# Three passes instead of two through the first expert's hidden blocks, fewer early weight tiles and fewer dummy matmuls

## The chip, the cores and the metric

The kernel runs on one core of one Trainium2 chip. The metric is device time in microseconds (us) of one execution, the median of several runs. One further execution is recorded by the hardware profiler, and all rows below come from that one.

## The reference, cut to what matters

```python
attn_out = _attn_ref(q, k, v, n_global, n_local)     # B=2, H=8, S=768, D=64
x = transpose(attn_out).reshape(1536, 512)           # tokens x model
x = _moe_ref(x, w_in, w_out)                         # d_ff = 2048
return _moe2_ref(x, w_gate, w_val, w_out2)           # d_ff = 1536

# _attn_ref: softmax(q k^T / 8 - slope * distance), keys kept if local (0 <= i - j < 96) or global (j < 8)
# _moe_ref:  h = x @ w_in;  g = h * tanh(softplus(h));  g @ w_out
# _moe2_ref: silu(x @ w_gate) * (x @ w_val) @ w_out
```

The weights are float64 and come as pairs of int32 words; the kernel turns them into float32 itself.

## The kernel before

**Stages.** The attention goes over 12 tiles of 128 tokens (6 for each of two batches), each in two halves of four heads. Then the first expert goes over 16 blocks of 128 hidden columns, then the second over 12. A chunk is 512 tokens, so there are three chunks (`NCH`). Every float32 operand of an expert's matmul is split in a high and a low part, and a product takes three matmuls (`PASSES`, `mm3`, L371).

**Attention, one half tile.** `transp` (L440) transposes q and k on TensorE into a PSUM bank of the pool `t_p`, and ACT or DVE evicts it to `kq`; `qk` (L469) makes the scores; `softmax` (L485) runs four biased minimum reductions on DVE (L499) and four exponentials on ACT (L329); `turn` (L528) transposes the exponentials through `t_p`, and ACT or DVE evicts them to `et`. Once for a tile, `spread` (L508) transposes the reciprocals through `t_p` into `rs`, and `pv` (L551) multiplies with the values into a bank of `t_p`. Of the eight PSUM banks the scores use banks 0 to 3, `t_p` banks 4 to 6, and `warm_p` bank 7 alone.

**Dummies.** `warm_up` (L590) makes `WARM` = 6 matmuls of 128x512 at the very start and `LATE` = 24 more of the lowest priority, which run wherever the planner sees TensorE free. All write bank 7.

**Weights.** `convert` (L392) loads one tile (512 KB from HBM), takes the absolute value of the high words on ACT (L404), runs four integer steps on DVE (L887 to L890), copies the high part to the tile on ACT or POOL (L352, L349) and subtracts for the low part on DVE (L362). A block of the first expert needs two tiles, `in` and `out`; a block of the second needs three. There are 13 slots `wa` from the start and 15 more, `wb`, once the attention's memory is given back (`switch`, L830). In the attention's loop `units_to(min(9, max(0, (s - 3)//2)))` (L827) writes nine conversions into the program, one for each two half tiles; all later ones are placed by `need` (L852), up to eight jobs ahead of their use.

**First expert.** `jobs_b` (L736) takes two blocks: `hidden` (24 matmuls, L681) into two banks `h`, then `mish` (L698: on ACT tanh, a table load, logarithm, a table load, tanh; on DVE a product and the split), then `out_b` (L759: 24 matmuls). The four output banks `y` are banks 4 to 7, given over when the attention is done (L841). The order is: blocks 0 to 7 for chunks 0, 1 and 2, then blocks 8 to 15 for chunks 0, 1 and 2 (`FA` = 8, L845). At the end of a chunk in the first pass the four `y` banks are copied to `st` and stored to `part1` in HBM (L779, L780); in the second they are loaded back (L782), added on DVE (L588) and split by POOL into the second expert's input. `st` has two slots, and two more (`sb`) after `switch`.

**Order.** Nothing runs in the order of the source. All operations go into `Plan` with assumed costs; `order` (L182) fills each engine's queue greedily, always with the ready operation of the lowest priority value, which is the due time worked back from its users. Engines then run these queues in order, each instruction waiting on its inputs. Copies that ACT, DVE or POOL can do are given to one of them there. A pool's buffers are handed out in the order of the source.

Of the kernel before, what the change touches and what calls it, by code (L numbers as in the profile page):

```python
# [13 lines left out]
ALU = mybir.AluOpType  # L14
# [205 lines left out]
def kernel(  # L220
# [14 lines left out]
    nc = tc.nc  # L235
# [6 lines left out]
    KD = DM // P  # L242
    CH = 512
    NCH = NTOK // CH
    FA = F1 // 2
    NWA = 13
    NWB = 15
    NST = 2
    WARM = 6
    LATE = 24  # L250
    EDGE = 104
    SPARE = 2500.0
    SCALE = -1.0 / float(D) ** 0.5
# [55 lines left out]
    sm_p = Pool(slots(asb, 3, [P, H], F32, "sm"))  # L309
    asb.tile([P, EDGE], I32, name="edge")  # L310

    asb_pools = [*raw_in.values(), e_p, sm_p, et_p, rb_p, xs_p, rs_p, t_p, warm_p]
    asb_fixed = [bias, bias0, kq, kg, mn, nt, nf, chk]

    def of_attention(o):
# [17 lines left out]
    def dve(emit, r, w, n=512, fast_=False):  # L333
        return op([("V", (150 if fast_ else 68) + (0.52 if fast_ else 1.045) * n, emit)], r, w)

    def dma(emit, r, w, kb=256, prio=None):
        return op([("S", 150 + kb * 4.2, emit)], r, w, lat=2000.0, prio=prio)
# [77 lines left out]
    def load(i, names="qk"):  # L415
        b, t = tiles[i]
        for nm, src in (("q", q), ("k", k), ("v", v)):
            if nm not in names:
                continue
            x = plan.buf(raw_in[nm])  # L420
            raws[nm, i] = x
            for hs in (slice(0, 4), slice(4, 8)) if i == 0 else (slice(0, H),):
                dma(lambda x=x, src=src, hs=hs: nc.sync.dma_start(
                    out=x.t[:, hs], in_=src[b, hs, t * P:(t + 1) * P, :].rearrange("h s d -> s h d")), [],
                    [(x, hf) for hf in range(hs.start // 4, hs.stop // 4)], kb=32 * (hs.stop - hs.start),
                    prio=-1e6 + hs.start + 9 * (nm == "v") if i == 0 else None)
# [160 lines left out]
    def tt(o, a, b_, op_):  # L587
        nc.vector.tensor_tensor(out=o, in0=a, in1=b_, op=op_)  # L588
# [13 lines left out]
    def setup():  # L602
        warm_up(WARM, LATE)
        load(0, "qk")
        op([("S", 154, lambda: nc.sync.dma_start(out=nt.t[:, 0:2], in_=n_global.bitcast(I32).partition_broadcast(P)))], [],
           [(nt, 0)], lat=3700.0, prio=-2e6)
        op([("S", 154, lambda: nc.sync.dma_start(out=nt.t[:, 2:4], in_=n_local.bitcast(I32).partition_broadcast(P)))], [],
           [(nt, 1)], lat=3700.0, prio=-2e6)
        load(0, "v")
        idb = Buf(t=ident)  # L610
        op([("G", 300, lambda: make_identity(nc, ident))], [], [(idb, 0)])
        op([("A", 1300, lambda: nc.scalar.preload_act_table_set(SET_EXP_TANH))], [], [(table, 0)])
        s0, s1 = plan.buf(e_p), plan.buf(e_p)
        v0 = lambda i, n: s0.t.rearrange("p a b -> p (a b)")[:, i:i + n]
        v1 = lambda i, n: s1.t.rearrange("p a b -> p (a b)")[:, i:i + n]
        rel_i, key_i = lambda: v0(0, 256).bitcast(I32), lambda: v0(256, 128).bitcast(I32)
        rel, key, neg, far = lambda: v0(384, 256), lambda: v0(640, 128), lambda: v0(768, 128), lambda: v1(0, 256)
        dist = (lambda: v1(256, 128), lambda: v1(384, 256))
        ng, nl = lambda: nf.t[:, 0:1], lambda: nf.t[:, 2:3]

        def iotas():
            nc.gpsimd.iota(rel_i()[:, 0:128], pattern=[[-1, 128]], base=128, channel_multiplier=1)
            nc.gpsimd.iota(rel_i()[:, 128:256], pattern=[[-1, 128]], base=0, channel_multiplier=1)
            nc.gpsimd.iota(key_i(), pattern=[[1, 128]], base=0, channel_multiplier=0)

        op([("G", 900, iotas)], [], [(s0, 0)])

        def distances():
            nc.vector.tensor_copy(rel(), rel_i())
            nc.vector.tensor_copy(key(), key_i())  # L630
            ts(neg(), rel()[:, 128:256], 0.0, ALU.is_lt, FAR, ALU.mult)
            tt(rel()[:, 128:256], rel()[:, 128:256], neg(), ALU.max)

        op([("V", 810, distances)], [(s0, 0)], [(s0, 1)])

        def masks():
            nc.vector.tensor_copy(nf.t, nt.t)
            ts(far(), rel(), nl(), ALU.is_ge, FAR, ALU.mult)
            tt(dist[1](), rel(), far(), ALU.max)
            ts(key(), key(), ng(), ALU.is_ge, FAR, ALU.mult)  # L640
            ts(key(), key(), nl(), ALU.max)
            tt(dist[0](), dist[1]()[:, 128:256], key(), ALU.min)
            nc.vector.tensor_copy(dist[1]()[:, 0:WG], key()[:, 0:WG])

        op([("V", 1800, masks)], [(nt, 0), (nt, 1), (s0, 1)], [(s1, 0), (nf, 0)])
        for o, c0, x, n in ((bias0, 0, dist[0], P), (bias, 0, dist[1], 2 * P), (bias, 2 * P, lambda: dist[1]()[:, 0:P], P)):
            for h in range(H):
                slope = 2.0 ** (-8.0 * (h + 1) / H)
                copy(lambda o=o, c0=c0, n=n, h=h: o.t[:, h, c0:c0 + n], x, [(s1, 0)], [(o, h)], scale=slope / SCALE, n=n)
# [109 lines left out]
    def out_b(kind, c, f, first, last, whole, g, w, ds):  # L759
        for d in ds:  # L760
            if first:
                ys[d] = plan.buf(y_p)
            y = ys[d]
            blk = slice(d * P, (d + 1) * P)

            def emit(y=y, blk=blk):
                if kind == 1:
                    mm3(y.t, lambda a: w.t[:, a, blk], lambda b: g.t[:, b, :], first, last)
                else:
                    mm3(y.t, lambda a: g.t[:, a, blk], lambda b: w.t[:, b, :], first, last)  # L770

            pe(emit, [(w, 0), (w, 1), (g, 0), (g, 1)], [(y, 0)], 3, CH, spare=SPARE)
            if not last:
                continue
            st = plan.buf(st_p)
            Y, T = [(y, 0)], [(st, 0)]
            if not whole:
                part, pk = (part1, p1) if kind == 1 else (part2, p2)
                copy(lambda st=st: st.t, lambda y=y: y.t, Y, T, scale=1.0 if kind == 1 else 0.5, psum_in=True, on="AV")  # L779
                dma(lambda st=st, d=d, part=part: nc.sync.dma_start(out=part[c, d], in_=st.t), T, [(pk, (c, d))])  # L780
            elif kind == 1:
                dma(lambda st=st, d=d: nc.sync.dma_start(out=st.t, in_=part1[c, d]), [(p1, (c, d))], T)  # L782
                dve(lambda st=st, y=y: tt(st.t, y.t, st.t, ALU.add), Y, T)
                ks = lambda a: [(xt[c], (a, d, t)) for t in range(CH // P)]
                copy(lambda d=d: xt[c].t[:, 0, d, :], lambda st=st: st.t, T, ks(0), on="G")
                arith(lambda d=d: xt[c].t[:, 1, d, :], lambda st=st: st.t,
                      lambda d=d: xt[c].t[:, 0, d, :].bitcast(F32), ALU.subtract, T + ks(0), ks(1), on="G")
            else:
                dma(lambda st=st, d=d: nc.sync.dma_start(out=st.t, in_=part2[c, d]), [(p2, (c, d))], T)
                dve(lambda st=st, y=y: nc.vector.scalar_tensor_tensor(out=st.t, in0=y.t, scalar=0.5, in1=st.t,  # L790
                                                                      op0=ALU.mult, op1=ALU.add), Y, T)
                r = c * CH + d * P
                dma(lambda st=st, r=r: nc.sync.dma_start(out=out[r:r + P, :], in_=st.t), T, [])


    setup()
    load(1)
    transp(0, 0)
    transp(0, 1)
# [2 lines left out]
    def units_to(n):  # L802
        while n_units[0] < min(n, len(units), freed[0] + room[0]):
            convert(n_units[0])
            n_units[0] += 1

    NS = 2 * NTL
    for s in range(NS + 2):
        i, hf = divmod(s, 2)
        if s < NS:  # L810
            if hf == 0:
                load_previous(i)
                if i + 1 < NTL:
                    load(i + 1, "v")
            qk(s)
            softmax(s)
            move_k(i, hf)
            if i + 1 < NTL:
                transp(i + 1, hf)
            if hf == 1 and i + 2 < NTL:  # L820
                load(i + 2)
        if 0 <= s - 1 < NS:
            turn(s - 1)
            if s % 2 == 0:
                spread(s // 2 - 1)
                pv(s // 2 - 1)
        units_to(min(9, max(0, (s - 3)//2)))  # L827
        if s == NS:
            flag()
    def switch():  # L830
# [11 lines left out]
       grow=[(w_p, wb_slots), (st_p, st_slots), (y_p, bank[4:8])])  # L842
    room[0] += NWB
    seq = []
    for fs, whole in ((range(0, FA), False), (range(FA, F1), True)):  # L845
        for c in range(NCH):
            seq += [(1, c, f, f == fs[0], f == fs[-1], whole) for f in fs]
    for fs, whole in ((range(0, F2 // 2), False), (range(F2 // 2, F2), True)):
# [281 lines left out]
```

## Time and profile before

| | us |
|---|---|
| median of 3 runs (669.0 to 670.03) | 669.59 |
| the profiled execution's own time | 668.81 |
| its span, first to last instruction | 667.0 |

The rows below are of that profiled execution. PE is TensorE's matmul side, PEld its weight loads, DVE VectorE, ACT ScalarE, POOL GpSimd, SPq the DMA issues of SyncE. The recorded durations of matmuls overlap, so the distance of starts, or a piece of the chain divided by its count, tells the cost of one. "Idle" is time before an instruction, with what ended it.

### The profile page before, as it was taken

Reading aid. Unit: us, or ns where it says so; the run is one execution under the profiler, and the core shown is the slowest. Engines: PE = TensorE matmul, PEld = TensorE weight load, DVE = VectorE, ACT = ScalarE, POOL = GpSimd, SP = SyncE. Lnnn points to the kernel's source line nnn. Section 1 sums busy time; section 2 is a strip of 40 time slices with the busy share of each in tenths; the row PEclk is TensorE's granted clock in tenths of the full one; section 3 lists DMA queues with packets and bytes.
Section 4 is the critical chain, followed back from the end, with each engine's and each line's share of the span. In section 5 each row is a group of like instructions: output and inputs, shape, how many; then the busy total and the mean of one; then the engine's idle time right before and its main releaser. Section 6 shows DMA issues by size and latency. Waiting matters only on the chain.

```text
span 667.0 us, 9142 instructions
## 1 busy us (share of the span) xinstructions
PE 652.8 (98%) x3343; PEld 535.9 (80%) x3343; DVE 410.5 (62%) x831; ACT 351.1 (53%) x636; POOL 109.7 (16%) x168
## 2 busy tenths in 40 slices
PE   8998999999999999999999999999999999999996
PEld 6876778878888888888888888888888888888884
DVE  5788887888678685797688877222842223323313
ACT  6999997878766776867685333212521211111111
POOL 4343542112111110150251410000000000000000
PEclk9999999999999999999999999999999999999999
DMA  8677641433325234243132224100400300300301
GB/s 197 171 174 179 168 129 63 127 127 130 117 70 179 73 132 153 94 143 124 51 127 93 97 70 142 72 1 1 148 10 16 111 0 17 111 0 17 110 1 68
DMA packets 80068, 63.58 MB, mean 95 GB/s; under 512 B 48272, under 2 KB 68752, under 8 KB 80016
## 3 DMA queue, kind: packets, MB, share of 16 engines
q1 hardware_dynamic: 80016, 62.93, 30.8%
q8 instruction: 28, 0.46, 0.3%
q14 instruction: 24, 0.20, 0.1%
HBM read 53.48 MB, written 9.44 MB: 94 GB/s over the span
## 4 chain that ended last, share of the span: by engine, by line
PE 89%; ACT 5%; DVE 2%; DMA 2%; issue 1%; SPq 0%; ACTq 0%; DVEq 0%
PE bank L373 78%; PE bank L562 3%; PE bank L480 3%; PE bank L541 2%; PE bank L451 2%; DMA raw<-in_moe_w_out_dram 1%; ACT e L329 1%; ACT et L352 1%; PE bank L596 1%; PE bank L522 1%; ACT kq L352 1%; ACT cv L404 1%; DMA in_k<-in_k_dram 1%; ACT u L329 0%; DVE a L362 0%
## 5 line engine op out<-in xcount | busy, mean ns | idle before, releaser
L373 PE MATMUL bank<-x,wa 128*128 128x512 f32 x756 | 180.8, 390 | 1.3 <-DVE a L362 1.3
L373 PEld LDWEIGHTS bank<-x,wa 128*128 128x128 f32 x756 | 141.7, 188 | 31.3 <-DVE a L362 1.7
L373 PE MATMUL bank<-x,wb 128*128 128x512 f32 x684 | 163.5, 390 | 0.0
L373 PEld LDWEIGHTS bank<-x,wb 128*128 128x128 f32 x684 | 128.4, 188 | 26.6
L329 ACT ACTIVATE u<-bank 128x512 f32<-128x512 f32 x84 | 49.9, 594 | 133.4 <-PE bank L373 133.2
L352 ACT ACTIVATE g<-a 128x512 fp32r<-128x512 f32 x64 | 40.3, 632 | 109.9 <-DVE a L729 93.7
L727 DVE SCALAR_TENSOR_TENSOR a<-u,bank 128x512 f32<-128x512 f32 x36 | 24.7, 687 | 92.0 <-ACT u L329 91.9
L362 DVE TENSOR_TENSOR g<-a,g 128x512 fp32r<-128x512 f32 x84 | 61.0, 738 | 22.5 <-ACT g L352 19.3
L373 PE MATMUL bank<-wa,g 128*128 128x512 f32 x288 | 70.2, 389 | 0.0
L373 PE MATMUL bank<-g,wb 128*128 128x512 f32 x288 | 69.0, 389 | 0.0
L373 PE MATMUL bank<-g,wa 128*128 128x512 f32 x288 | 68.9, 390 | 0.0
L373 PEld LDWEIGHTS bank<-g,wa 128*128 128x128 f32 x288 | 54.1, 188 | 11.2
L373 PEld LDWEIGHTS bank<-g,wb 128*128 128x128 f32 x288 | 54.1, 188 | 11.2
L373 PEld LDWEIGHTS bank<-wa,g 128*128 128x128 f32 x288 | 54.1, 188 | 11.2
L729 DVE TENSOR_TENSOR a<-a,bank 128x512 f32<-128x512 f32 x36 | 24.7, 687 | 49.4 <-PE bank L373 49.3
L889 DVE SCALAR_TENSOR_TENSOR cv<-raw,cv 128x512 int32<-128x512 int32 x68 | 48.4, 717 | 0.9
L404 ACT ACTIVATE cv<-raw 128x512 f32<-128x512 f32 x68 | 44.8, 665 | 7.7 <-DMA raw<-in_moe_w_out_dram 4.6
L887 DVE TENSOR_SCALAR cv<-cv 128x512 f32<-128x512 f32 x68 | 35.0, 516 | 22.3 <-ACT cv L404 22.1
L890 DVE SCALAR_TENSOR_TENSOR cv<-raw,cv 128x512 int32<-128x512 int32 x68 | 47.5, 706 | 0.8
L329 ACT ACTIVATE e<-e,mn 128x256 f32<-128x256 f32 (+1 forms) x96 | 46.1, 490 | 1.1 <-DVE mn L499 0.8
L349 POOL TENSOR_SCALAR g<-a 128x512 fp32r<-128x512 f32 x20 | 13.2, 659 | 202.6 <-DVE a L729 125.8
L362 DVE TENSOR_TENSOR a<-bank,u 128x512 f32<-128x512 f32 x48 | 31.1, 686 | 18.9 <-ACT u L329 18.4
(92 smaller groups left out, 748.0 us busy)
## 6 DMA issues: line engine op xcount, KB each, us to landing
raw<-in_moe_w_out_dram SPq DMA_DIRECT2D x28, 512.0 KB, 3.3
raw<-in_moe_w_in_dram SPq DMA_DIRECT2D x16, 512.0 KB, 3.8
raw<-in_moe_w_gate_dram SPq DMA_DIRECT2D x12, 512.0 KB, 3.7
raw<-in_moe_w_val_dram SPq DMA_DIRECT2D x12, 512.0 KB, 3.6
part<-st SPq DMA_DIRECT2D x12, 256.0 KB, 2.1
part<-sb SPq DMA_DIRECT2D x12, 256.0 KB, 2.1
st<-part SPq DMA_DIRECT2D x12, 256.0 KB, 2.8
sb<-part SPq DMA_DIRECT2D x12, 256.0 KB, 3.7
```

The costliest lines, as they stand in the source:

```text
L329: nc.scalar.activation(out=o(), in_=i(), func=func, scale=scale, **args)
L352: lambda: nc.scalar.activation(out=o(), in_=i(), func=AF.Copy, scale=scale)),
L362: return lambda: eng.tensor_tensor(out=o(), in0=x(), in1=y(), op=alu)
L373: nc.tensor.matmul(out=o, lhsT=lhs(a), rhs=rhs(b), start=first and i == 0, stop=last and i == len(PASSES) - 1)
L404: op([("A", 520, lambda: nc.scalar.activation(out=wf(), in_=hi().bitcast(F32), func=AF.Abs))], R, W_)
L480: nc.tensor.matmul(out=banks[j].t[:, p * 256:p * 256 + nb * P], lhsT=kq.t[ro, pr, 2, :], rhs=kq.t[ro, pr, 0:nb, :].rearrange("p b s -> p ( ...
L562: nc.tensor.matmul(out=o.t[64 * j:64 * j + 64, p * P:(p + 1) * P], lhsT=v_of(c).t[:, 2 * p + j, :], rhs=et4[p].t[:, c, j, :], start=c == 0 ...
L727: dve(lambda: nc.vector.scalar_tensor_tensor(out=a.t, in0=u.t[:, 0], scalar=1.0, in1=hg.t, op0=ALU.add, op1=ALU.mult), U + [(hg, 0)], A_)
L729: dve(lambda: nc.vector.tensor_tensor(out=a.t, in0=a.t, in1=hv.t, op=ALU.mult), [(hv, 0)], A_)
L887: lambda: ts(out=f(), in0=f(), scalar1=F64_LOW, scalar2=F64_HIGH, op0=ALU.max, op1=ALU.min),
L889: lambda: stt(out=w(), in0=high(), scalar=-0x40000000, in1=w(), op0=ALU.bitwise_and, op1=ALU.bitwise_or),
L890: lambda: stt(out=w(), in0=low(), scalar=29, in1=w(), op0=ALU.logical_shift_right, op1=ALU.bitwise_or),
```

## The change

The first expert goes in three passes, over blocks 0 to 3, 4 to 7 and 8 to 15, each for all chunks. The middle pass loads the partial sum, adds and stores it back. The attention's loop writes five conversions instead of nine, starting two half tiles later. Six late dummies stay of 24, and an operation without instructions hands bank 7 to `t_p` after the last dummy, so that the attention has four banks there.

```diff
-    FA = F1 // 2
+    PASSES1 = (0, 4, 8)
...
-    LATE = 24
+    LATE = 6
...
-    asb_pools = [*raw_in.values(), e_p, sm_p, et_p, rb_p, xs_p, rs_p, t_p, warm_p]
+    asb_pools = [*raw_in.values(), e_p, sm_p, et_p, rb_p, xs_p, rs_p, t_p]
...
-            if not whole:
+            if kind == 1 and whole == 1:
+                dma(lambda st=st, d=d: nc.sync.dma_start(out=st.t, in_=part1[c, d]), [(p1, (c, d))], T)
+                dve(lambda st=st, y=y: tt(st.t, y.t, st.t, ALU.add), Y, T)
+                dma(lambda st=st, d=d: nc.sync.dma_start(out=part1[c, d], in_=st.t), T, [(p1, (c, d))])
+            elif not whole:
...
     setup()
+    op([("X", 0, lambda: None)], after=[o for o in plan.ops if any(b.pool is warm_p for b in o.bufs)], lat=0.0, prio=0.0,
+       grow=[(t_p, bank[7:8])])
...
-        units_to(min(9, max(0, (s - 3)//2)))
+        units_to(min(5, max(0, (s - 5) // 2)))
...
-    for fs, whole in ((range(0, FA), False), (range(FA, F1), True)):
+    for n, f0 in enumerate(PASSES1):
+        fs = range(f0, (PASSES1 + (F1,))[n + 1])
+        whole = (n > 0) + (fs[-1] == F1 - 1)
```

## Rows read from the trace of the kernel before

**Rows 1.** The page's part 1: busy time and share of the span by engine.
```profile
PE 652.8 (98%) x3343; PEld 535.9 (80%) x3343; DVE 410.5 (62%) x831; ACT 351.1 (53%) x636; POOL 109.7 (16%) x168
```
**Rows 2.** The chain that ended last, in order of time: start, length, what.
```profile
99.60 5.70 PE bank L373 x24
...
148.88 511.69 PE bank L373 x2256
```
**Rows 3.** Stretches: length, busy PE, PEld, DVE, ACT, POOL (instructions), granted clock, DMA.
```profile
10.00:44.00 34.00, 34.00 (x314) 26.91 (x312) 27.25 (x103) 32.04 (x108) 13.40 (x31) 1.00 0.75 188
44.00:100.00 56.00, 51.96 (x516) 40.99 (x511) 47.15 (x173) 52.59 (x166) 24.87 (x42) 1.00 0.64 161
100.00:150.00 50.00, 48.70 (x246) 39.92 (x245) 41.97 (x75) 38.51 (x50) 8.89 (x12) 1.00 0.33 106
```
**Rows 4.** Waits of PE, whole run: total us, times, longest.
```profile
PE bank L541 <- ACT kq L352: 1.1, 2, 0.8
...
PE bank L373 <- DVE a L362: 1.3, 1, 1.3
```
**Rows 5.** The chain again, within the attention: TensorE's pieces of one tile, `spread` of others.
```profile
25.63 0.44 PE bank L522 x4
...
70.25 0.44 PE bank L541 x4
...
72.34 0.44 PE bank L522 x4
72.78 1.06 PE bank L480 x8
73.84 1.90 PE bank L562 x32
75.74 0.59 PE bank L451 x4
...
80.63 0.44 PE bank L522 x4
```
**Rows 6.** Dummies (L596) in one stretch; and a group of four on the chain.
```profile
10.50:42.00 31.50, 6.61 (x19) 2.90 (x17) 1.00 0.79 199
...
15.73 0.94 PE bank L596 x4
```
**Rows 7.** Stretches counting only DVE's instructions on the conversions' tile `cv`, then ACT's.
```profile
10.00:100.00 90.00, 28.23 (x42) 1.00 0.68 171
...
10.00:100.00 90.00, 6.07 (x9) 1.00 0.68 171
```
**Rows 8.** ACT's evictions to `et`, 10 to 100 us: busy, mean ns, idle before.
```profile
L352 ACT ACTIVATE et<-bank 128x512 f32<-128x512 f32 (+1 forms) x45 | 23.4, 556 | 2.0 <-PE bank L541 1.7
```
**Rows 9.** DVE's additions of a loaded partial sum at the end of a chunk.
```profile
L588 DVE TENSOR_TENSOR sb<-bank,sb 128x512 f32<-128x512 f32 x6 | 3.8, 680 | 0.0
```
**Rows 10.** Timeline: last step of converting tiles 8, 9, 10 on DVE; matmuls on PE.
```profile
103.21 0.68 DVE L362 TENSOR_TENSOR wa<-cv,wa 128x512 fp32r<-128x512 f32 x1
...
109.43 0.69 DVE L362 TENSOR_TENSOR wa<-cv,wa 128x512 fp32r<-128x512 f32 x1 [0.74 <-POOL wa L349]
...
111.89 5.76 PE L373 MATMUL bank<-x,wa 128*128 128x512 f32 x24
...
120.03 0.68 DVE L362 TENSOR_TENSOR wa<-cv,wa 128x512 fp32r<-128x512 f32 x1
```
**Rows 11.** Timeline of PE: transposes of q and k early and late.
```profile
6.00 0.42 PE L451 MATMUL bank<-ident,in_q 128*128 128x128 f32 x1
6.21 0.42 PE L451 MATMUL bank<-ident,in_k 128*128 128x128 f32 x1
...
69.76 0.27 PE L451 MATMUL bank<-ident,in_q 128*128 128x128 f32 x1
69.87 0.27 PE L451 MATMUL bank<-ident,in_k 128*128 128x128 f32 x1
```

## The prediction, made before the changed kernel was run

> **What bounds the kernel now.** I began with the shares of the span: PE is busy 98% of it, ACT 53%, DVE 62% [rows 1]. Such a share only says that TensorE is the engine to follow; matmuls overlap in the records, so it doesn't say that TensorE is saturated everywhere. So next I read the chain of work that ended last. From 148.88 us on it is one piece, 511.69 us for 2256 expert matmuls, 0.2268 us each, to the end [rows 2]. No wait breaks it: over that stretch the kernel is bound by the count of matmuls, and the change keeps this count (16 x 3 x 24 in the first expert and 12 x 3 x 36 in the second, 2448). All that can be won or lost lies in front of it. The 192 expert matmuls before 148.88 cost 192 x 0.2268 = 43.5 us; the other 105.4 us are start, attention, dummies and waits.
>
> Third, the stretches. In the attention ACT is busy 32.04 of 34 us and then 52.59 of 56 us, together 84.6 of 90, or 94%. PE has no idle time to 44 us and 56 - 51.96 = 4.0 us after that [rows 3], the longest of them put down to an eviction by ACT [rows 4]. From 100 to 150 us PE idles 1.3 us in a single wait, for DVE's product of `mish`, just ahead of the unbroken piece [rows 3, 4].
>
> Fourth, one attention tile. `spread` stands at 25.63 and, seven tiles later, at 80.63: 7.86 us a tile. TensorE's own work in a tile, from the chain's pieces, is two `qk` (2 x 1.06), four halves of `turn` (4 x 0.44), two `transp` (0.59 behind `pv`, else 0.44), `spread` 0.44 and `pv` 1.90: 7.25 us [rows 5]. ACT's is 94% of 7.86, 7.39 us. So two engines with queues in order are both close to full, and neither gets to its own floor: ACT loses 0.47 us a tile, and PE 0.61, to dummies at first and to waits later.
>
> **The change, part by part.**
>
> *Dummies.* 18 of 24 late ones go. They run from the start on as holes come up, 30 in all, and from 10.5 us on the trace counts 19, two of them begun just before [rows 6]. So the 12 that remain would be used up at about that point, and the removal falls on the time behind it, to 42 us. A group of four is 0.94 us of the chain, 0.235 us each, so 18 hold 4.2 us of PE's queue. It isn't all won: they stand where the planner saw PE waiting, and where ACT is the later engine PE will wait there instead. Bounds 0 and 4.2 us; I count them together with ACT's load below, for neither comes free without the other.
>
> *Early conversions, nine to five.* One conversion costs ACT 6.07 / 9 = 0.67 us and DVE 28.23 / 42 x 5 = 3.4 us [rows 7]. Four fewer relieve the attention of 2.7 us of ACT and 13.4 us of DVE. They are not gone: tiles 5, 6 and 7 are needed soon behind it, and the planner may slip them into the attention's last tiles. So ACT has five to eight conversions there instead of nine over some 11.4 tiles (from 10 to 100 us): 0.30 to 0.47 us a tile against 0.53. DVE has room to take a few of the 45 evictions to `et` that ACT does at 0.56 us each [rows 8]; I count one in four tiles, 0.14, since DVE takes few of them now although it is idle for 8.85 of 56 us [rows 3]. (The Trainium skill, "TensorEngine Tiling (Array Packing)", section "PSUM Bottleneck", says to use both ScalarE and VectorE for PSUM evacuation. By that rule the 13.4 us that DVE is relieved of would go to evictions, ACT would be clear of TensorE's floor, and the attention would give the upper bound below; the rows agree with it so far only in a few.) ACT then stands at 7.39 - 0.06 to 0.23 - 0.14, that is 7.0 to 7.2 us, level with or a little below TensorE's 7.25.
>
> *The bank.* A fourth bank in `t_p` lets TensorE write one more transposition before an eviction is done; the wait named above is of this kind. It has no instruction. What it buys is how near the later of two engines comes to its floor. Today that is 94%. If it stays at 94%, a tile takes 7.25 / 0.94 = 7.71 us, and 11.4 tiles gain 1.7 us; at 100% they take 7.25 and gain 7.0 us. Bounds 1.7 and 7.0. I take 97%, 7.47 us, half way, because two kinds of obstruction go at once (dummies and evictions queued behind conversions) but both engines stay nearly full: **4.5 us**. The dummies' 4.2 us and the 4.0 us of idle time are inside of it, and their sum, 8.2, is the most that the attention can give.
>
> *Three passes.* With four blocks in the first pass, chunk 0 takes 4 x 24 x 0.2268 = 21.8 us and needs eight tiles, and chunks 1 and 2 use them again for 43.5 us; before, chunk 0 asked for 16 tiles in 43.5 us. In the old order DVE is at 41.97 of 50 us from 100 to 150 [rows 3], and the wait of 1.3 us is its being late there. With eight tiles due within 65 us in place of sixteen within 43.5, `mish` no longer stands behind integer steps. So that wait goes: **1.3 us**, bounds 0 and 1.3. What is late next is tile 6 or 7 (a rival below).
>
> *The middle pass's extra work.* 12 loads, 12 additions and 12 stores of 256 KB are added. An addition is 0.68 us on DVE [rows 9]: 8.2 us in 65 us, beside matmuls. The old second pass has the same edges (load, add, then POOL's split) inside the unbroken 511.69 us [rows 2], and its loads are issued long ahead. What no row shows is such edges every 21.8 us instead of 43.5. A bank `y` is used again only after the rest of the pair and the next pair's `hidden`, 18 + 24 matmuls, 9.5 us. Bounds 0 and one exposed addition at each of three edges, 2.0 us. I take 0, as in the nearest rows. On SP's queue the loads and stores wait for `st` slots and for the additions, and weight loads are queued behind them; these have a pass of slack now. The hand-over of bank 7 adds no wait that anyone queues behind: the last dummy is past by about 11 us.
>
> **Sum.** 4.5 + 1.3 - 0 = 5.8 us. The profiled execution, 668.81 us (span 667.0 and 1.8 around it), would become 663.0. It lies 0.8 below the median of the runs shown, which I take as the base: 669.59 - 5.8 = **663.8 us**. With the ends: least gain 1.7 + 1.3 - 2.0 = 1.0, or 668.6; greatest 8.2 + 1.3 = 9.5, or 660.1.
>
> **The rivals.**
>
> *The gap refills.* The planner never leaves an engine idle when something is ready, so it may run the same conversions at the same places, only under a later due time; ACT stays as full as it is and PE waits where dummies stood. For it: ACT is at 94% now, and eight slots `wa` more are free than the five tiles take. Against it: in the old trace tile 9, the first one placed by its need, is finished only at 109.43 [rows 10], so low urgency did mean late. Then only the wait goes: 669.59 - 1.3 = 668.3 us. Chance 0.14.
>
> *Tiles 5 to 7 come late.* Slower. If they are converted only when ACT is through with the attention, the old rows for the next three tiles are the model: 103.21, 109.43 and 120.03 [rows 10], 4.5 earlier 98.7, 104.9 and 115.5. TensorE wants tile 7 after the first pair's 24 `hidden`, the 12 of block 2, the 24 begun at 111.89 [rows 10] and the first pair's 24 `out` matmuls, at 122.8, or 118.3 in new time: 2.8 us to spare. It decides when two of the intervals are as long as the longer one, 10.6 us: then the last tile comes at 98.7 + 21.2 = 119.9, and if the first is late by as much too, at 127.6. That is 9.3 us late, and 669.59 - 5.8 + 9.3 = 673.1 us. Against it: TensorE can do the next chunk's `hidden` with tiles that are there. Chance 0.09, a third of it small enough to end at no change.
>
> *The clock falls.* Without dummies PE's queue has holes between 14 and 42 us. At half clock two transposes start 0.21 us apart (6.00 and 6.21), at full clock 0.11 [rows 11]. One tile at half clock costs about 7.25 - 0.61 = 6.6 us, 670.4; all to 42 us some 23 us, 686. Against it: from 44 to 100 us there is not one dummy, PE idles 4.0 us, and the granted clock is 1.00 throughout, 2.4 GHz [rows 3]. The Trainium skill, "TensorE: Matmul & The Clock Gate", section "A second HAM failure mode: psum-queue depth-cycling", tells of a kernel whose banks were cycled and whose TensorE idled briefly and often between groups of matmuls, so that its clock went up and down. By that rule the attention without dummies would be such a case and the second price due. This trace differs: at 69.76 us, 28 us after the last dummy and among waits of up to 0.8 us [rows 4], transposes still start 0.11 us apart. Chance 0.05.
>
> **How the numbers follow.** Forecast 0.72, from 660.1 to 667.9; refill 0.14 (0.05 of it just past the line to faster); late tiles 0.09; clock 0.05. About 0.2%, 1.3 us, is what a measurement of this kernel can tell from no change. Faster 0.72 + 0.05 = 0.77; same 0.09 + 0.03 = 0.12; slower 0.06 + 0.05 = 0.11. The range from 660.0 to 668.6 takes in the unknown costs and the refill.
>
> **What would show it.** Right: `spread` of successive tiles about 7.5 us apart, ACT at 96% or more and fewer than seven conversions in the attention, no wait over 0.3 us behind it, the unbroken piece of expert matmuls starting with the first pair, still 0.2268 us each. Wrong: the same 7.86 us a tile with PE idle in place of dummies; a wait of `hidden` or `out` for a weight tile soon after the attention; transposes 0.21 us apart after 11 us; waits at the middle pass's edges.

## The result

The changed kernel takes 659.25 us (659.16 to 659.38) beside 669.5 for the old one on the same chip: ratio 0.985, 95% interval 0.9837 to 0.9864. It is faster by 10.25 us where 5.8 was forecast, and 0.75 us below the range. The profiled executions differ by 668.81 - 659.16 = 9.65 us, so 0.6 of the miss is the old kernel's own spread (the runs shown reach from 669.0 to 670.03) and the rest is real.

First the shares and the chain in order of time, as in rows 1, 2 and 5:

```profile
PE 647.0 (98%) x3325; PEld 532.4 (81%) x3325; DVE 420.2 (64%) x846; ACT 350.5 (53%) x638; POOL 110.1 (17%) x163
```
```profile
23.19 0.59 PE bank L522 x4
...
74.44 0.59 PE bank L522 x4
...
92.58 5.51 PE bank L373 x24
...
99.39 2.77 PE bank L373 x12
...
104.17 546.98 PE bank L373 x2412
```

The unbroken piece now begins with the third run of expert matmuls, at 104.17, and has 2412 of them at 0.2268 us. The same matmuls were broken once before. In the timeline, the view of rows 10, they began at 111.89, and now at 104.10:

```profile
104.10 6.21 PE L373 MATMUL bank<-x,wa 128*128 128x512 f32 x26
```

So the 9.65 us are 7.8 for the attention, 1.3 for the wait [rows 4], and some 0.5 in rests of 0.1 to 0.3 us that I didn't trace. Seven tiles from the second `spread` to the ninth take 51.25 us, 7.32 each, where TensorE's own work is 7.25 [rows 5]. Here are these seven tiles as a stretch, before and after (columns as in rows 3):

```profile
25.63:80.63 55.00, 52.23 (x516) 41.45 (x514) 46.29 (x157) 51.17 (x161) 22.45 (x41) 1.00 0.70 172
```
```profile
23.19:74.44 51.25, 50.48 (x509) 40.58 (x510) 44.95 (x160) 48.80 (x158) 25.91 (x43) 1.00 0.74 182
```

The stretches of rows 3, then PE's waits as in rows 4, then all instructions on `cv` as in rows 7 (here to the end of the attention at 92 us, DVE, ACT, POOL):

```profile
10.00:44.00 34.00, 32.99 (x324) 26.46 (x323) 28.71 (x111) 32.05 (x111) 15.07 (x31) 1.00 0.81 201
44.00:100.00 56.00, 55.23 (x525) 44.58 (x525) 49.92 (x174) 52.19 (x163) 27.16 (x43) 1.00 0.57 142
100.00:150.00 50.00, 50.00 (x245) 41.27 (x244) 37.96 (x67) 40.87 (x53) 8.67 (x11) 1.00 0.29 97
```
```profile
PE bank L522 <- ACT et L352: 0.5, 1, 0.5
PE bank L541 <- DVE xs L570: 0.5, 1, 0.5
PE bank L480 <- ACT kq L352: 0.5, 1, 0.5
```
```profile
10.00:92.00 82.00, 22.45 (x32) 4.61 (x7) 4.26 (x6) 1.00 0.70 174
```

PE idles 0.8 us between 44 and 100 where it idled 4.0, and not at all from 100 to 150. From 10 to 44 us, where dummies had filled every hole, it now idles 1.0 us. ACT is as busy as it was, 84.2 of 90 us. Seven absolute values fall before 92 us: TensorE is quicker without ACT being emptier.

Evictions on DVE from 10 to 92 us, of the old kernel and then of the changed one; then, of the changed kernel, the dummies of rows 6, the additions of rows 9, the last steps of tiles 5 and 7 as in rows 10, and transposes as in rows 11:

```profile
L349 DVE TENSOR_SCALAR rs<-bank 128x512 f32<-128x512 f32 x5 | 3.4, 688 | 1.2 <-ACT et L352 1.0 <-PE bank L522 0.3
L349 DVE TENSOR_SCALAR kq<-bank 128x512 f32<-128x512 f32 x4 | 2.8, 692 | 2.0 <-PE bank L451 1.3 <-ACT e L329 0.5
```
```profile
L349 DVE TENSOR_SCALAR et<-bank 128x512 f32<-128x512 f32 x7 | 4.7, 689 | 2.5 <-PE bank L541 1.7 <-ACT e L329 0.8
L349 DVE TENSOR_SCALAR kq<-bank 128x512 f32<-128x512 f32 x6 | 4.1, 685 | 0.3 <-PE bank L451 0.3
L349 DVE TENSOR_SCALAR rs<-bank 128x512 f32<-128x512 f32 x4 | 2.7, 684 | 0.2 <-ACT e L329 0.2
```
```profile
L596 PE MATMUL bank<-g x12: 628/628/792, 1.5 to 8.3; 128*128 128x512 f32 x12
```
```profile
L588 DVE TENSOR_TENSOR sb<-bank,sb 128x512 f32<-128x512 f32 x12 | 8.1, 688 | 0.0
```
```profile
95.75 0.64 DVE L362 TENSOR_TENSOR wa<-cv,wa 128x512 fp32r<-128x512 f32 x1
...
104.82 0.68 DVE L362 TENSOR_TENSOR wa<-cv,wa 128x512 fp32r<-128x512 f32 x1
```
```profile
17.91 0.27 PE L451 MATMUL bank<-ident,in_k 128*128 128x128 f32 x1
18.02 0.27 PE L451 MATMUL bank<-ident,in_q 128*128 128x128 f32 x1
```

DVE now does 17 evictions instead of nine, seven of them to `et`. The last dummy starts at 8.3. Tile 7 is there at 104.82, well ahead of the 115 us or so at which TensorE wants it (the forecast's reckoning less 7.8). Ten microseconds after the last dummy the transposes stand 0.11 us apart: full clock.

### The profile page after: what moved, and what is told of

Read it like the earlier page. It is cut to its first block, busy times and chain, and to the rows that moved or that the text cites. A ratio compares the mean times of both kernels' runs of the same rounds, so it can differ in the third digit from the quotient of the medians.

```text
span 657.4 us, 9143 instructions
## 1 busy us (share of the span) xinstructions
PE 647.0 (98%) x3325; PEld 532.4 (81%) x3325; DVE 420.2 (64%) x846; ACT 350.5 (53%) x638; POOL 110.1 (17%) x163
## 4 chain that ended last, share of the span: by engine, by line
PE 95%; ACT 2%; DMA 1%; POOL 0%; DVE 0%; SPq 0%; issue 0%; ACTq 0%
PE bank L373 84%; PE bank L562 3%; PE bank L541 3%; PE bank L480 3%; PE bank L451 2%; ACT e L329 1%; PE bank L522 1%; DMA in_k<-in_k_dram 1%; ACT bias L352 0%; ACT kq L352 0%; ACT et L352 0%; POOL sm L512 0%; POOL rb L516 0%; DVE sb L794 0%; POOL x L349 0%
## 5 line engine op out<-in xcount | busy, mean ns | idle before, releaser
L349 POOL TENSOR_SCALAR g<-a 128x512 fp32r<-128x512 f32 x21 | 16.3, 776 | 209.2 <-DVE a L729 131.0
L895 DVE TENSOR_SCALAR cv<-cv 128x512 f32<-128x512 f32 x68 | 32.5, 483 | 19.8 <-ACT cv L404 19.7
```

What stands on the lines that cost most here:

```text
L895: lambda: ts(out=f(), in0=f(), scalar1=F64_LOW, scalar2=F64_HIGH, op0=ALU.max, op1=ALU.min),
```

## The experiments

Each row is one kernel with its median beside that of the old kernel on the same chip. The last column is where the piece that runs unbroken to the end begins in its profile: its last 2412 matmuls, or as many as the brackets say where a wait comes later.

| kernel | edit | us | old kernel | ratio, 95% | unbroken from |
|---|---|---|---|---|---|
| old | | 669.5 | | | 148.88 (2256) |
| changed | | 659.25 | 669.5 | 0.985, 0.9837 to 0.9864 | 104.17 |
| a_twopass | two passes again | 676.21 | 668.82 | 1.0114, 1.0097 to 1.0131 | 152.77 (2256) |
| a_late24 | 24 late dummies again | 663.35 | 669.23 | 0.9918, 0.9901 to 0.9934 | 107.55 |
| a_nobank | bank 7 not handed over | 664.57 | 669.23 | 0.9934, 0.9918 to 0.9951 | 109.33 |
| a_late24_nobank | both | 665.65 | 669.23 | 0.9952, 0.9936 to 0.9969 | 109.51 |
| a_units9 | nine conversions, old places | 664.72 | 669.23 | 0.9934, 0.9918 to 0.9951 | 109.68 |
| b_threepass | old, three passes | 667.36 | 669.13 | 0.9975, 0.9965 to 0.9984 | 111.92 |
| b_late6 | old, 6 late dummies | 672.02 | 669.13 | 1.0043, 1.0026 to 1.006 | 150.49 (2256) |
| b_late6_bank | old, 6 late dummies, bank | 675.57 | 669.13 | 1.0105, 1.008 to 1.013 | 153.77 (2256) |
| b_units5 | old, five conversions, later | 680.9 | 669.13 | 1.0173, 1.0156 to 1.019 | 158.65 (2256) |
| a_pass4_12 | passes of 4 and 12 | 673.9 | 668.82 | 1.0076, 1.0059 to 1.0093 | 239.41 (1872) |
| a_late8 | 8 late dummies | 661.19 | 668.82 | 0.989, 0.9871 to 0.991 | 106.20 |
| a_late0 | no late dummies | 663.18 | 668.75 | 0.9913, 0.9895 to 0.9931 | 108.70 |
| a_shift6 | conversions half a tile later | 661.94 | 668.82 | 0.99, 0.9883 to 0.9916 | 106.31 |
| a_shift4 | half a tile sooner | 662.27 | 668.75 | 0.9904, 0.9887 to 0.9922 | 106.77 |
| a_units6 | six conversions | 660.3 | 668.75 | 0.9871, 0.9853 to 0.9888 | 104.72 |
| a_units4 | four | 658.74 | 668.75 | 0.985, 0.9832 to 0.9867 | 103.13 |
| a_units3 | three | 658.33 | 669.03 | 0.9842, 0.9825 to 0.986 | 103.36 |
| a_units9late | nine, changed kernel's start | 660.78 | 669.03 | 0.9879, 0.9862 to 0.9897 | 105.42 |

Since the old kernel's median moves by 0.75 us between chips, losses below are differences of the gains over it.

**One part undone.**

```diff
# a_late24
-    LATE = 6
+    LATE = 24
# a_nobank (warm_p goes back into asb_pools as well)
-    op([("X", 0, lambda: None)], after=[...warm_p...], lat=0.0, prio=0.0, grow=[(t_p, bank[7:8])])
# a_units9
-        units_to(min(5, max(0, (s - 5) // 2)))
+        units_to(min(9, max(0, (s - 3)//2)))
```

> The changed kernel (659.25 us) with the 24 late dummies back; bank 7 still goes to the attention, but only after the last of them. Theory 'dummies' (18 of them at 0.235 us stood in TensorE's queue between 10 and 42 us and delayed what was ready): +4.2 us, 663.5. Theory 'bank' (the fourth bank is what lets TensorE run on; the dummies only filled holes): it comes some 30 us later, so about a third of its worth is lost, +1 to +2.5 us, 660.3 to 661.8. Theory 'conversions' (fewer of them unload ACT): no loss, 659.3.

> The changed kernel with bank 7 left unused after the last dummy, so three banks for the attention's transposes as before. Theory 'bank': the 4.0 us of TensorE's waits from 44 to 100 us come back, and some in the first half, +4 us or more, 663 to 665. Theory 'dummies': +0 to +1.5 us, 659.3 to 660.8. Theory 'conversions': +0 to +1 us.

> The changed kernel with both undone, 24 late dummies and three banks; conversions and passes stay changed. If dummies and bank carry the attention's gain of 7.8 us, this is 659.25 + 7.8 = 667 us, and the two losses measured singly add up to it unless each needs the other. Theory 'conversions' (four conversions fewer in the attention relieve ACT of 2.7 us and DVE of 13.4): it keeps at least 2.7 us of the 7.8, 664 us or less.

> The changed kernel with nine early conversions again, one for each two half tiles from the fifth on. Theory 'conversions': +2.7 us (ACT's share of four conversions) to +5 us, 662 to 664.3. Theories 'dummies' and 'bank': +0 to +1.5 us, since the lead over the old kernel was 6.1 us by the time of `spread` for tile 6, at 59 us, where the number of conversions differed by one.

The dummies cost 4.4 us when they come back, the missing bank 5.6, both together 6.7, the nine conversions 5.7. The first two are what the theory of their own part said, the third lies 0.4 us above its theory's range, and both together lie between the two theories. The three losses can't all be right by adding: 4.4 + 5.6 + 5.7 is twice the 7.8 us that there are. The traces tell where each arises. In a_nobank and a_units9 the second `spread` is where the changed kernel has it (23.01 and 23.12 us, beside 23.12 in the timeline), and the seven tiles behind it take 55.0 and 55.5 us again. In a_late24 the first `spread` is 5.2 us later (21.21 instead of 16.02), of which 3.4 are left where the unbroken piece begins. So the dummies cost at the start, and the quick pace is lost with the bank as well as with the nine conversions at their old places. How much of each loss is the part's own stays open: the neighbours below lose up to 3.8 us by edits with hardly any work in them.

Without the bank the waits return as the prediction named them, on evictions:

```profile
PE bank L522 <- ACT et L352: 2.2, 5, 0.7
```

**One part alone on the old kernel.**

```diff
# b_late6
-    LATE = 24
+    LATE = 6
# b_late6_bank: the same, and warm_p out of asb_pools, and after setup()
+    op([("X", 0, lambda: None)], after=[...warm_p...], lat=0.0, prio=0.0, grow=[(t_p, bank[7:8])])
# b_units5
-        units_to(min(9, max(0, (s - 3)//2)))
+        units_to(min(5, max(0, (s - 5) // 2)))
# b_threepass: PASSES1 = (0, 4, 8) and the branch for whole == 1 alone
```

> The old kernel (669.5 us) with 6 late dummies instead of 24, nothing else. Theory 'complements' (TensorE, ACT's evictions and the banks are all close to full, and freeing one alone leaves the others as the bound): 0 to -1.5 us, 668 to 669.5. Theory 'dummies' (they cost their 4.2 us wherever they stand): 665.3 us. Theory 'lottery' (any edit gives the greedy planner another order, better or worse by some us, whatever the edit means): any sign, -4 to +4.

> The old kernel with 6 late dummies and bank 7 handed to the attention. The changed kernel with nine early conversions took 664.72 us and has the three passes besides, so the two-pass order here should add the 1.3 us wait: 666 us. Theory 'complements': 665 to 667. Theory 'lottery': no relation, 662 to 672.

> The old kernel with five early conversions, later by two half tiles, nothing else. The first chunk still asks for 16 weight tiles in 43.5 us, now with four fewer ready. Theory 'complements': the attention ends 0 to 2 us sooner, but DVE is late behind it by up to four conversions, 13 us of its time spread over 50 us, so more waits of the 1.3 us kind: 669 to 675 us. A rival, that the conversions behind the attention have room: 667.5 us.

> The old kernel with the three passes of 4, 4 and 8 blocks, nothing else. The prediction's step: the 1.3 us wait goes and the middle pass costs nothing, 668.2 us. If the extra edges cost an exposed addition each, 2.0 us more: 670.2. Theory 'lottery' allows nothing for the attention here unless its order changes: -2 to +2 besides.

On the old kernel fewer dummies alone lose 2.9 us, with the bank 6.4, and the fewer conversions 11.8; the passes alone gain 1.8. The bank was not tried alone. b_late6_bank and b_units5 came out slower than any theory allowed (675.57 beside 672, 680.9 beside 675). Here are the first pair's `hidden` and the last unbroken piece of b_late6, then the last unbroken piece of b_units5 and that of b_threepass:

```profile
97.11 5.67 PE bank L373 x24
...
150.49 513.27 PE bank L373 x2256
```
```profile
158.65 514.37 PE bank L373 x2256
```
```profile
111.92 546.98 PE bank L373 x2412
```

In b_late6 the first pair starts 2.5 us sooner than in rows 2, and the last piece 1.6 us later. TensorE waits for a product of `mish` again, now 4.1 us, and the last piece itself takes 1.6 us longer for the same 2256 matmuls (2.7 in b_units5): behind such waits the clock is low, as the next group shows. What the attention saves is lost here. Ahead of the product DVE stands idle for 5.67 us, and the product starts as ACT's last tanh ends (b_late6):

```profile
148.67 1.04 ACT L329 ACTIVATE u<-u 128x1024 f32<-128x1024 f32 x1
```
```profile
148.80 0.43 DVE L887 TENSOR_SCALAR cv<-cv 128x512 f32<-128x512 f32 x1 [5.67 <-ACT cv L404]
...
149.75 1.29 DVE L362 TENSOR_TENSOR a<-bank,u 128x512 f32<-128x512 f32 x2
```

So here it is ACT that is late, with two `mish` one behind the other and a conversion's absolute value in front of the last tanh; DVE has room. With three passes the wait is gone, at the old attention's pace.

**The passes undone, and another way to have a short first one.**

```diff
# a_twopass
-    PASSES1 = (0, 4, 8)
+    PASSES1 = (0, 8)
# a_pass4_12
+    PASSES1 = (0, 4)
```

> The changed kernel (659.25 us) with two passes of eight blocks again. The attention is as quick as changed, but 16 weight tiles are due within 43.5 us, eleven of them not ready. Theory 'passes enable' (with two passes the time is set by when DVE has made the tiles of the first pass, and a quicker attention only waits longer for them): the old kernel with five early conversions took 680.9 us, and this one about the same, 677 to 683. The prediction's step, by which the passes are worth one wait of 1.3 us: 660.6 us.

> The changed kernel with two passes of 4 and 12 blocks: the first pass is as short, the middle pass's 12 loads, additions and stores are gone, but the second pass wants 24 weight tiles within its first chunk, 65 us. If the middle pass costs nothing and is needed for nothing: 659.3 us. If DVE can't make 24 tiles in time (28 slots, eight of them held by the first pass to its end): waits between 170 and 235 us, 660 to 668. If the extra edges cost something: 657 to 659.

With two passes the changed kernel has its quick attention (first pair at 92.13) and loses 17.6 us. Its waits, three stretches of it with the granted clock, and its chain:

```profile
PE bank L373 <- DVE a L362: 8.4, 2, 4.6
```
```profile
132.00:136.00 4.00, 3.06 (x7) 2.51 (x8) 3.30 (x7) 2.18 (x4) 0.00 (x0) 0.50 0.78 254
136.00:152.00 16.00, 12.99 (x54) 10.31 (x52) 7.42 (x13) 12.72 (x15) 1.29 (x2) 0.93 0.23 68
152.00:157.00 5.00, 4.23 (x10) 3.40 (x11) 4.97 (x10) 2.44 (x4) 0.00 (x0) 0.50 0.01 3
```
```profile
92.13 5.50 PE bank L373 x24
...
132.94 7.90 PE bank L373 x24
...
152.77 514.15 PE bank L373 x2256
```

Two waits for `mish`, 8.4 us together, and behind each a stretch at a granted clock of 0.50, 1.2 GHz, in which 24 matmuls take 7.90 us instead of 5.50. With 2.4 us of this behind each wait they make some 13 of the 17.6 us. The second wait is for ACT, as in b_late6. In the first the product stands in DVE's queue behind the steps of two conversions, 2.5 us after its tanh has ended:

```profile
128.65 1.05 ACT L329 ACTIVATE u<-u 128x1024 f32<-128x1024 f32 x1
```
```profile
131.00 1.28 DVE L898 SCALAR_TENSOR_TENSOR cv<-raw,cv 128x512 int32<-128x512 int32 x2
132.20 0.68 DVE L362 TENSOR_TENSOR a<-bank,u 128x512 f32<-128x512 f32 x1
```

Passes of 4 and 12 move the trouble to the second pass, which wants 24 tiles within one chunk. At 673.9 us this kernel is slower than its expectation allowed (668 at most):

```profile
206.38 0.80 PE L373 MATMUL bank<-g,wb 128*128 128x512 f32 x1 [3.80 <-POOL g L349]
...
239.41 4.61 PE L373 MATMUL bank<-x,wa 128*128 128x512 f32 x12 [4.35 <-DVE a L362]
```

So the middle pass isn't overhead that one could leave out, in either way that was tried. By the count it keeps the demand for tiles at eight in each 65 us, 27 us of DVE at 3.4 us each [rows 7], and gives time to get ahead for the third pass. Other divisions into passes were not run.

**Neighbours of the changed kernel.** These ask whether its order is a lucky one.

```diff
# a_late8, a_late0
+    LATE = 8          # or 0
# a_shift6, a_shift4
+        units_to(min(5, max(0, (s - 6) // 2)))     # or s - 4
# a_units6, a_units4, a_units3, a_units9late
+        units_to(min(6, max(0, (s - 5) // 2)))     # or 4, 3, 9
```

> The changed kernel with 8 late dummies instead of 6. Two more dummies are 0.47 us of TensorE's queue and keep bank 7 a few us longer. Theory 'complements' (each part frees an engine that is nearly full): 659.3 to 660.5 us. Theory 'lottery' (any edit gives the greedy planner another order, and the changed kernel's is a lucky one): 661 to 666 us.

> The changed kernel with the five early conversions one half tile later, nothing else. No work is added or removed in the attention. Theory 'complements': 658.5 to 660 us. Theory 'lottery': 661 to 666 us.

> The changed kernel (659.25 us) with no late dummy at all: bank 7 comes to the attention a few us sooner, and TensorE's holes before 9 us stay empty. Theory 'complements': 658.5 to 659.5. Theory 'order' (a term of about 2 us either way that any edit draws anew, as 1.9 and 2.7 us in the runs with 8 dummies and with the later conversions): 660 to 663. If the dummies are needed for the clock at the start: two transposes 0.21 us apart for longer than to 9.6 us, +1 to +3 us.

> The changed kernel with the five early conversions one half tile sooner. Theory 'complements': 659 to 660.5 us. Theory 'order': 660 to 663 us, as one half tile later gave 661.9.

> The changed kernel with six early conversions instead of five. Theory 'complements': a quarter of the 5.5 us that nine cost, 660.6 us. Theory 'order': anything from 658 to 663 us.

> The changed kernel with four early conversions instead of five. Theory 'complements' (each conversion out of the attention frees ACT and DVE): 657.9 to 659.3, as nine to five gave 5.5 us or 1.4 us each, with no wait behind the attention as long as tile 4 is there for block 2. Theory 'order': 660 to 663 us.

> The changed kernel (659.25 us) with nine early conversions, but starting as late as the changed kernel's five. It splits the 5.5 us that nine conversions at the old places cost (664.7) into their number and their place. Theory 'number' (4 conversions at the 1.1 us that six against five showed): 663.5 to 664.7. Theory 'place' (one half tile's shift alone cost 2.7 to 3.0 us in two runs): 660 to 662.

> The changed kernel with three early conversions. Theory 'number': one conversion fewer than four gains again up to 1 us, 657.7 to 658.7, if TensorE finds other work while tile 4 is made. If tile 4 is late for block 2's `hidden` (it starts some 7 us after the first pair's): a wait of 1 to 4 us, 660 to 663.

Three edits with hardly any work in them cost 2.6 us (two more dummies), 3.4 and 3.8 us (half a tile later or sooner). The number of conversions matters little when they start where the changed kernel starts them: against it three, four, six and nine give -0.45, +0.2, +1.8 and +2.0 us. Nine at the old places cost 5.7, so 3.7 of that is place; with the later start the seven tiles keep the quick pace (51.2 us). The changed kernel and a_shift6 in two stretches of the attention (PE is the first busy figure):

```profile
10.00:59.00 49.00, 47.99 (x480) 38.51 (x478) 41.88 (x164) 46.17 (x160) 21.91 (x42) 1.00 0.77 187
59.00:92.00 33.00, 32.23 (x327) 25.71 (x326) 29.56 (x98) 31.04 (x99) 17.23 (x27) 1.00 0.59 154
```
```profile
10.00:59.00 49.00, 48.30 (x481) 38.88 (x482) 42.37 (x164) 46.20 (x159) 21.95 (x45) 1.00 0.78 189
59.00:92.00 33.00, 30.02 (x294) 23.94 (x292) 29.68 (x98) 31.65 (x101) 13.34 (x25) 1.00 0.58 153
```

To 59 us they run alike; after it the later conversions leave PE idle for 3.0 us of 33 instead of 0.8, with the same load on ACT and DVE. That is order, not work. Of the seven neighbours that keep six or eight late dummies, the middle one is 2.0 us behind the changed kernel. Three and four conversions are within the measurement of five, so nothing here clearly beats the changed kernel.

## Why the prediction was right or wrong

*What bounds it, and the side.* Right: the unbroken piece kept its 0.2268 us a matmul, and all was won ahead of it.

*The bank and the 97%.* This is the step that failed, a term mis-sized: 4.5 us forecast, 7.8 measured. It assumed that two engines near their floors hold TensorE to 97% of its own, evenly over 11.4 tiles. Over the seven tiles TensorE came to 7.25 / 7.32 = 99% and idled 0.77 us in all. ACT was where the forecast had it, at 48.80 / 7 = 6.97 us a tile (forecast 7.0 to 7.2) and 95% full, and still cost TensorE almost nothing. So these tiles gave 3.8 us where 0.39 a tile makes 2.7. Nor was the gain even. 2.4 us came before the second `spread` (25.63 to 23.19), where 4.1 us of dummies had stood on the old chain behind 10 us, and the forecast has 0.8 for two tiles; 1.6 us came behind the ninth, forecast 1.0.

Why two queues so full hardly held each other back is not shown. DVE took more evictions than the one in four tiles that I gave it: 17 to `et`, `kq` and `rs` between 10 and 92 us, from nine. The Trainium skill, "TensorEngine Tiling (Array Packing)", section "PSUM Bottleneck", by which both engines should evict and which would have given the upper bound, was nearer than my weighing of it. But the count alone doesn't set the pace: a_shift4 has 17 such evictions too and loses 3.8 us. About 2.0 us of the 7.8 may be the good order that the neighbours show, that is luck; without it the kernel would be near 661.3, inside the range. This share is an estimate from seven neighbours, four of which change the number of conversions as well, and not proved.

*The range's low end.* I put the most that the attention can give at 8.2 and the wait at 1.3, and the sum, 9.5, held for the profiled execution but for 0.15 us. Taken off the median 669.59 it left no room for the medians' own spread. That, not a mechanism, puts 659.25 outside; the forecast within the range missed by the term above.

*Dummies and conversions counted inside one term.* Right that the gains don't add, but the split was guessed. Dummies back cost 4.4 us, near their 4.2 us of queue, at the start of the attention; conversions were given 2.7 us of ACT, and their number is worth 2.0 (nine against five from the same start).

*The passes.* "That wait goes" came true, and b_threepass shows it (1.8 us), but its reason was only half read. The prediction has DVE late there, with `mish` behind integer steps. In the old chain the product follows ACT:

```profile
146.47 0.68 ACT cv L404
147.16 0.95 ACT u L329
148.13 0.70 DVE a L362
```

ACT's tanh, behind a conversion's absolute value, ends at 148.11, and DVE starts the product at 148.13. DVE's integer steps end at 148.08, so taking these away alone would have gained nothing. Fewer conversions within the first chunk relieve both engines, so the wait went all the same. Its worth was wrong for the new kernel: undone there, it is 17.6 us. A wait in the old trace prices the removal only while nothing else moves; here the other three parts each change when TensorE comes to the same products of `mish`. The prediction treated the parts' terms as if they could be added, and they came out as near the sum as they did only because the passes were among them.

*The middle pass's edges.* Right: 12 additions more at 0.69 us, and no wait.

*The rivals.* The refill didn't come: seven absolute values fell before 92 us, but PE's holes closed. Late tiles didn't come with three passes. With two, in b_units5 (11.8 us slower) and a_twopass, TensorE waits 8.4 us for products of `mish`, which stand behind conversions on ACT or DVE, and at most 0.6 us for a tile itself. That the rival's price, 9.3 us, was near them is chance, as it was worked out for tiles 5 to 7. The granted clock stayed at 1.00 from 10 to 150 us with 12 dummies.

*What would show it.* Right were the early unbroken piece (with the attention's last pieces between its first runs, and no wait), the 0.2268 us and the missing wait behind the attention. The tiles were 7.32 us apart, not 7.5. ACT at 96% or more was wrong, it stayed at 94% from 10 to 100 us and came to 95% in the seven tiles; and fewer than seven conversions were expected, against seven begun.

## What to carry to other kernels

Before a wait is priced from the trace, ask what else in the change brings work to it sooner: a part that looks worth 1.3 us can be what lets the others pay at all, and a part that speeds up the stage ahead can cost more than it gives while that queue stands. Where a planner makes the order, run a few neighbours that change next to nothing, and take their spread, here 2 to 4 us of 659, as the size below which a part's effect isn't its own; by that measure much of the 4.4 to 5.7 us of the single parts here is open. Two engines that are both near full need not hold each other back: here one at 95% cost the other under 2%. And before a wait is put down to the engine that released it, read what that engine had waited for.

## What the runs showed of the hardware that was not expected

The clock fell in two ways. In the dense expert matmuls of the five kernels with long waits (a_twopass, a_pass4_12, b_late6, b_late6_bank, b_units5), single waits of 3.3 to 4.6 us brought the granted clock to 0.50 behind them, and slower matmuls for a few microseconds, so that such a wait costs more than its length; the 1.3 us wait of the old kernel brought none [rows 2, 3]. And in a_late0, with the six early dummies only, the transposes were at full clock at first and at half from 8 us on:

```profile
5.88 0.27 PE L451 MATMUL bank<-ident,in_q 128*128 128x128 f32 x1
5.99 0.27 PE L451 MATMUL bank<-ident,in_k 128*128 128x128 f32 x1
...
8.33 0.42 PE L451 MATMUL bank<-ident,in_q 128*128 128x128 f32 x1
8.55 0.42 PE L451 MATMUL bank<-ident,in_k 128*128 128x128 f32 x1
```
```profile
8.00:15.00 7.00, 5.95 (x29) 4.39 (x30) 2.47 (x17) 5.00 (x22) 4.02 (x13) 0.52 0.91 206
```

Before it fell, TensorE had run the six dummies to 4.4 us and then stood idle for 1.35, 0.69 and 0.39 us between a few transposes and scores. The granted clock was 0.52 from 8 to 15 us, and the first `spread` came at 17.73 instead of 16.02, 1.7 us of the 4.7 that this kernel loses; the other 3.0 are within what a neighbour's order costs. The changed kernel's transposes stand 0.21 us apart too, but earlier: at 5.99 and 6.20, as in the old kernel [rows 11], and 0.11 apart before 10 us. Its granted clock reads 1.00 there, so at the very start the distance of transposes and that column don't agree. The six late dummies probably pay for themselves, then; the eighteen behind them cost 4.4 us.
